# Own due times for the quarter products of two nested block products, other planning constants, one more sum by adding transfers, 19 warm-up products and a re-cut first block

## The chip, the cores and the metric

The kernel runs on one core of a Trainium2 chip. In the profile's words the core has PE (TensorE, the matrix engine; PEld are its weight loads), DVE (VectorE), ACT (ScalarE), POOL (GpSimd) and SP (SyncE, which here only issues transfers). Each engine takes its instructions in program order and waits on semaphores for the others. Transfers that SP, ACT and POOL issue run on 16 shared DMA engines. Operands lie in SBUF, products in eight PSUM banks of 128 x 512 floats. The metric is the device time of one execution in microseconds (us).

## The reference

```python
g = sigmoid((x * gate_w).sum(-1, keepdims=True))           # x: 2048 x 1024
a = x @ dft_hid_re.T;  b = x @ dft_hid_im.T
A = dft_seq_re @ a - dft_seq_im @ b                        # 2048 x 1024
h = layernorm(x)                                           # over the 1024 columns
u = gelu(h.T @ w1 + b1)                                    # 1024 x 3584
B = (u @ w2 + b2).T                                        # 2048 x 1024
out = g * A + (1 - g) * B
```

All inputs and the output are float32.

## The kernel before

Four stages follow each other: `Fourier` (names begin with q: the sequence transforms of x), `Mixed` (y: the hidden transforms of q, into the output), `Up` (u: normalised x times w1, gelu) and `Down` (o: times w2, added into the output). Each stage is a product of two matrices whose operands W and R are cut into blocks. A bilinear scheme of 26 block products (`SCHEME`) takes the place of the 32 that blocks of 4 x 4 and 4 x 2 would need: for each product j (in names p0 to p25, by its place in the stage's order) sums of blocks are made on DVE (L539 adds, L542 subtracts), multiplied, and the result is added from PSUM onto up to eight blocks of the output (`q_c`, `u_c`, ... ; L907 and L909 copy on ACT or DVE the first time, L915 adds on DVE afterwards). Sums that are needed again are kept in DRAM and loaded again.

A float32 block is split into a rounded part hi (ACT, L572; in the first block partly DVE, L570) and a rest lo = v - hi (DVE, L579, or L577 when the sign turns). PE multiplies hi x hi, lo x hi and hi x lo into the same PSUM bank (L863, L864, L865; L982 in the first block). One block product in stage q is four steps k = 0 to 3 along the contraction, each 4 x 2 banks x 3 products.

Stage q has three specialities that the change touches. (1) In its first product, p0, step k = 0 is cut by columns (`first`, L935), so that PE can begin on a part: W comes in columns 0:128, 128:256 and 256:512, R in 0:256, 256:512 and 512:1024. (2) Products p9 and p22 (`Q_NEST`) are computed by `nested` (L995): the block product is cut once more into seven quarter products (tags 1, 5, 6, 2, 7, 3, 4, L1040) in banks X, T, Z and V, with sums of quarters (`q_p22_r_s1`, `q_p22_w_t1`, ...) made on DVE. (3) For products in `Q_DMA` a sum of two R blocks isn't made on DVE: POOL issues a transfer that adds a block from DRAM onto the one in SBUF (`add_onto`, L548). There are four such transfers of 512 KB per product, one for each k.

Nothing in the code fixes the order of the instructions by hand. Every operation is a task of `Graph` with an engine, a cost in us and a key (the step of the product it belongs to). `dues` (L330) walks back from the order of the PE tasks and gives each task a time by which it has to be done: the due time of what uses it, less its own cost, less `WAIT`, and less `LOAD` for a transfer or `HOP` otherwise; a task may not be due later than five us after its key's step on PE, whatever uses it. `schedule` (L360) then plays the program through with assumed durations (a transfer takes its bytes / `DMA_RATE` one after the other, plus `DMA_LATENCY`); each engine takes, of the tasks that are ready and have a buffer, the one due first. Buffers are 40 slots of 4 KB per partition ("f") and 23 of 2 KB ("h"). An "h" tile may take an "f" slot (`has_slots`, L385) only if it is first in line and one "f" is free. The order that comes out is the order in which each engine gets its instructions.

At its start PE runs 13 products of constants (`warm_up`, L1379), which nothing reads.

Of the kernel before, what the change touches and what calls it, by code (L numbers as in the profile page):

```python
# [14 lines left out]
P = 128  # L15
# [123 lines left out]
Q_DMA = (23,)  # L139
# [147 lines left out]
class Graph:  # L287
# [72 lines left out]
    def schedule(self):  # L360
# [113 lines left out]
def gated_mix_kernel(  # L474
# [444 lines left out]
    class Fourier(Bilinear):  # L919
# [15 lines left out]
        first = {"W": [(0, P), (P, P), (2 * P, 2 * P)], "R": [(0, 2 * P), (2 * P, 2 * P), (H, H)]}  # L935

        def block(self, x_, b, j, k, key):

            if (j, k) != (0, 0):
                return super().block(x_, b, j, k, key)  # L940
            src, r = self.source(x_, b, k)
            b = Buf("f" if x_ == "R" else "h", f"q_{x_}{b}_p0_0", None, 3)
            for i, (c, n) in enumerate(self.first[x_]):
                load(-18 + 2 * i, View(b, c, n, i), src[:, c:c + n], queue="ACT" if x_ == "W" and i < 2 else "SP")
            return View(b, 0, self.n[x_])

# [12 lines left out]
        def matmuls(self, j, ks, ops, eps):  # L959

            if j or ks[0] > 1:
                return super().matmuls(j, ks, ops, eps)
            (rh, rl), (wh, wl) = ops[0]
            hh, hl, lh = (wh, rh), (wh, rl), (wl, rh)
            if ks == (0,):
                for m in range(4):
                    for n in range(2):
                        self.PS[m, n] = View(Buf("ps", f"ps_q_p0_{m}_{n}"), 0, H)
                todo = [(hh, (0,), 0, 1), (lh, (0,), 0, 1), (hh, (1,), 0, 1), (hh, (0, 1), 1, 2), (lh, (1,), 0, 1), (lh, (0, 1), 1, 2),
                        (hl, (0, 1), 0, 1), (hl, (0, 1), 1, 2), (hh, (2, 3), 0, 2), (hl, (2, 3), 0, 2), (lh, (2, 3), 0, 2)]  # L970
                todo += [(p, (0, 1, 2, 3), 2, 4) for p in (hh, lh, hl)]
            else:
                todo = [(p, (0, 1, 2, 3), n, n + 2) for n in (0, 2) for p in (hh, hl, lh)]
            fresh = {(m, n) for m in range(4) for n in range(2)} if ks == (0,) else set()
            for (w, r), ms, a, b in todo:
                some = [(m, self.PS[m, a // 2], (m, a // 2) in fresh) for m in ms]
                fresh -= {(m, a // 2) for m in ms}

                def go(_, w=w, r=r, a=a, b=b, some=some):
                    c0 = a // 2 * H  # L980
                    for m, bank, begin in some:
                        nc.tensor.matmul(bank.buf.t[:, a * 2 * P - c0:b * 2 * P - c0], w.ap[:, m * P:(m + 1) * P],  # L982
                                         r.ap[:, a * 2 * P:b * 2 * P], start=begin, stop=False, skip_group_check=True)

                wp = tuple(sorted({min(m, 2) for m in ms})) if ks == (0,) else None
                rp = (2 if a == 2 else tuple(range(a, b))) if ks == (0,) else None
                g.add({"PE": (0.227 if b - a == 2 else 0.12) * len(ms)}, step, go, r=((w.buf, wp), (r.buf, rp)),
                      w=[q.reg for _, q, _ in some])
# [6 lines left out]
        def nested(self, j):  # L995
# [3 lines left out]
            key, name = step, f"{self.name}_p{j}"  # L999
# [40 lines left out]
            def product(tag, bank, begin, end=False):  # L1040
                rv, wv = made_r[tag], made_w[tag]
                rh, rl = parts("R", tag, rv, [1, 1])
                wh, wl = parts("W", tag, wv, [a[1] * b[1] for a, b in zip(rv, wv)])
                for m, ps in enumerate(banks[bank]):

                    def go(_, m=m, ps=ps):
                        for i in range(2):
                            wc, rc = slice((2 * i + m) * P, (2 * i + m + 1) * P), slice(i * H, i * H + H)
                            for w, r in ((wh, rh), (wh, rl), (wl, rh)):
                                nc.tensor.matmul(ps.ap, w.ap[:, wc], r.ap[:, rc], start=begin and i == 0 and (w, r) == (wh, rh),  # L1050
                                                 stop=end and i == 1 and w is wl, skip_group_check=True)

                    g.add({"PE": 1.36}, step, go, r=(rh.buf, rl.buf, wh.buf, wl.buf), w=(ps.reg,))
# [11 lines left out]
            def out(c, i):  # L1065
                at = 2 - 2 * (c in "VT")
                for m, ps in enumerate(banks[c]):
                    self.PS[at + m, int(c in "XT")] = ps
                    self.read(j, at + m, int(c in "XT"), step + i, 1)

            product("1", "X", True)
            copy("X", banks["Z"])
            s1, t1 = plus("s1", "R", r21, r22), plus("t1", "W", w12, w11, True)
# [305 lines left out]
    def warm_up(_):  # L1379
        for n in range(13):  # L1380
            nc.tensor.matmul(pw.t[:, :2 * P], ones[:, :P], ones[:, :2 * P], start=True, stop=True)

    g.add({"PE": 3.0}, 0, warm_up, w=(pw,))
# [61 lines left out]
```

## Time and profile before

| | |
|---|---|
| runs (median of 3) | 1846.67 us (1847.55, 1846.67, 1846.49) |
| profiled execution, own time | 1847.67 us |
| its span, first to last instruction | 1845.9 us |
| busy: PE, DVE, ACT, POOL | 1838.4, 1716.2, 923.3, 246.9 us |
| granted TensorE clock | 1.000 |
| DMA | 491.89 MB, mean 266 GB/s over the span |

The profile shows one execution. Names in it are without numbers: `q_p_w_lo` stands for the lo part of W in any product of q. A row of the timeline has the start, the length, engine, line, operation, out<-in, the shape and the count of equal instructions merged into it, and in brackets the idle time before it and who ended it. Consecutive matmuls overlap by design: one of 512 columns is shown as 389 ns long, but the next starts 227 ns after it, and a busy PE is not one without delays. `PEq`, `SPq`, `POOLq` are queues that issue.

### The profile page before, as it was taken

The numbers are of one execution on the slowest core, as the hardware profiler recorded it, in microseconds if no ns is written. First come the engines' busy times: TensorE is split into PE (matmuls) and PEld (weight loads), VectorE is DVE, ScalarE is ACT, GpSimd is POOL, SyncE is SP. The second block draws the span as 40 slices with busy tenths as digits, with TensorE's granted clock in tenths as the row PEclk, the third lists the DMA queues.
The fourth block names the chain that finished last, engine by engine and source line by source line (L and its number), as shares of the span: only waits on it lengthen the run. The fifth ranks groups of instructions, "written<-read, shape, count | busy, mean of one in ns | idle before, by whom it ended". The sixth has DMA issues, their size and how long they took to land.

```text
span 1845.9 us, 24510 instructions
## 1 busy us (share of the span) xinstructions
PE 1838.4 (100%) x8113; PEld 1520.6 (82%) x8113; DVE 1716.2 (93%) x2506; ACT 923.3 (50%) x1444; POOL 246.9 (13%) x420
## 2 busy tenths in 40 slices
PE   9999999999999999999999999999999999999999
PEld 7888888888788888888888888888888888888887
DVE  8899899989999999999997799899899999989996
ACT  5443545644645545586554434355465435444543
POOL 0100010011122101112121211121120000001111
PEclk9999999999999999999999999999999999999999
DMA  9956577978799867989658798996998665675973
GB/s 372 351 196 266 200 286 288 349 256 332 240 327 311 254 195 256 329 293 323 240 190 298 266 334 322 333 375 219 368 311 276 175 223 179 208 210 141 287 196 85
DMA packets 200447, 491.89 MB, mean 266 GB/s; under 512 B 24768, under 2 KB 25792, under 8 KB 200320
## 3 DMA queue, kind: packets, MB, share of 16 engines
q1 hardware_dynamic: 161424, 371.88, 58.5%
q0 software_dynamic: 38464, 118.25, 19.7%
q8 instruction: 63, 1.03, 0.2%
q14 instruction: 64, 0.52, 0.1%
q10 hardware_dynamic: 432, 0.20, 0.0%
HBM read 375.41 MB, written 114.82 MB: 266 GB/s over the span
## 4 chain that ended last, share of the span: by engine, by line
PE 93%; DVE 4%; DMA 2%; issue 0%; ACT 0%; SPq 0%; DVEq 0%
PE ps_u_p L865 9%; PE ps_u_p L864 9%; PE ps_u_p L863 9%; PE ps_o_p L863 9%; PE ps_o_p L864 9%; PE ps_o_p L865 9%; PE ps_q_p L864 6%; PE ps_q_p L865 6%; PE ps_q_p L863 6%; PE ps_y_p L865 5%; PE ps_y_p L863 5%; PE ps_y_p L864 5%; PE ps_q_p_X L1050 1%; DVE q_p_r_lo L579 1%; DVE q_c L915 1%; DMA q_R_p<-q_R 1%
## 5 line engine op out<-in xcount | busy, mean ns | idle before, releaser
L864 PE MATMUL ps_u_p<-u_p_r_lo,u_p_w_hi 128*128 128x512 f32 x728 | 283.2, 389 | 0.0
L863 PE MATMUL ps_u_p<-u_p_r_hi,u_p_w_hi 128*128 128x512 f32 x728 | 283.2, 389 | 0.0
L865 PE MATMUL ps_u_p<-u_p_r_hi,u_p_w_lo 128*128 128x512 f32 x728 | 283.2, 389 | 0.0
L863 PE MATMUL ps_o_p<-o_p_r,o_p_w 128*128 128x512 f32 x726 | 282.5, 389 | 0.1
L865 PE MATMUL ps_o_p<-o_p_r,o_p_w 128*128 128x512 f32 x726 | 282.4, 389 | 0.0
L864 PE MATMUL ps_o_p<-o_p_r,o_p_w 128*128 128x512 f32 x726 | 282.4, 389 | 0.0
L863 PE MATMUL ps_q_p<-q_p_r_hi,q_p_w_hi 128*128 128x512 f32 x592 | 230.3, 389 | 0.0
L864 PE MATMUL ps_q_p<-q_p_r_lo,q_p_w_hi 128*128 128x512 f32 x592 | 230.3, 389 | 0.0
L865 PE MATMUL ps_q_p<-q_p_r_hi,q_p_w_lo 128*128 128x512 f32 x592 | 230.3, 389 | 0.0
L572 ACT ACTIVATE q_p_r_hi<-q_R_p 128x1024 fp32r<-128x1024 f32 (+1 forms) x104 | 102.8, 1002 | 133.2 <-DVE q_R_p L539 97.8
L572 ACT ACTIVATE u_p_w_hi<-u_W_p 128x896 fp32r<-128x896 f32 x104 | 97.9, 950 | 139.2 <-DVE u_W_p L539 39.9
L572 ACT ACTIVATE o_p_r<-o_R_p 128x512 fp32r<-128x512 f32 x175 | 107.4, 626 | 113.0 <-DVE o_R_p L542 36.9
L572 ACT ACTIVATE o_p_w<-o_W_p 128x512 fp32r<-128x512 f32 x182 | 111.8, 626 | 102.4 <-PE ps_o_p L865 38.4
L863 PE MATMUL ps_y_p<-y_p_r,y_p_w 128*128 128x512 f32 x416 | 162.1, 390 | 0.0
L864 PE MATMUL ps_y_p<-y_p_r,y_p_w 128*128 128x512 f32 x416 | 161.9, 389 | 0.0
L865 PE MATMUL ps_y_p<-y_p_r,y_p_w 128*128 128x512 f32 x416 | 161.8, 389 | 0.0
L864 PEld LDWEIGHTS ps_u_p<-u_p_r_lo,u_p_w_hi 128*128 128x128 f32 x728 | 136.6, 188 | 28.5
L863 PEld LDWEIGHTS ps_u_p<-u_p_r_hi,u_p_w_hi 128*128 128x128 f32 x728 | 136.6, 188 | 28.3
L865 PEld LDWEIGHTS ps_u_p<-u_p_r_hi,u_p_w_lo 128*128 128x128 f32 x728 | 136.6, 188 | 28.3
L863 PEld LDWEIGHTS ps_o_p<-o_p_r,o_p_w 128*128 128x128 f32 x726 | 136.3, 188 | 28.7 <-DVE o_c L915 0.5
L865 PEld LDWEIGHTS ps_o_p<-o_p_r,o_p_w 128*128 128x128 f32 x726 | 136.3, 188 | 28.5
L864 PEld LDWEIGHTS ps_o_p<-o_p_r,o_p_w 128*128 128x128 f32 x726 | 136.3, 188 | 28.1
(229 smaller groups left out, 3641.4 us busy)
## 6 DMA issues: line engine op xcount, KB each, us to landing
q_R_p<-in_ct_dram SPq DMA_DIRECT2D x127, 512.0 KB, 7.7
u_W_p<-in_w_dram SPq DMA_DIRECT2D x136, 448.0 KB, 6.3
o_W_p<-in_w_dram SPq DMA_DIRECT2D x196, 256.0 KB, 5.1
o_R_p<-u SPq DMA_DIRECT2D x140, 256.0 KB, 4.4
u<-u_c POOLq DMA_DIRECT2D x126, 256.0 KB, 5.9
y_W_p<-q SPq DMA_DIRECT2D x99, 256.0 KB, 5.1
q<-q_c POOLq DMA_DIRECT2D x80, 256.0 KB, 6.1
q_W_p<-in_x_dram SPq DMA_DIRECT2D x75, 256.0 KB, 7.2
```

Source lines behind the costliest of these rows:

```text
L572: g.add({"ACT": act(v.n)}, key, lambda e: nc.scalar.activation(hi.ap, v.ap, AF.Copy, scale=-1.0 if negate else 1.0), r=(v.reg,), w=(hi.reg,))
L579: nc.vector.tensor_sub(lo.ap, v.ap, hi.ap.bitcast(F32))
L863: nc.tensor.matmul(bank.ap, wh.ap[:, c], rh.ap[:, e], start=a, stop=False, skip_group_check=True)
L864: nc.tensor.matmul(bank.ap, wh.ap[:, c], rl.ap[:, e], start=False, stop=False, skip_group_check=True)
L865: nc.tensor.matmul(bank.ap, wl.ap[:, c], rh.ap[:, e], start=False, stop=b, skip_group_check=True)
L915: lambda e: nc.vector.scalar_tensor_tensor(o.ap, ps.ap, scale, o.ap, op0=ALU.mult, op1=ALU.add),
L1050: nc.tensor.matmul(ps.ap, w.ap[:, wc], r.ap[:, rc], start=begin and i == 0 and (w, r) == (wh, rh), stop=end and i == 1 and w is wl, skip_g ...
```

## The change

Five edits go together.

- The planner's constants: `HOP` 0.3 to 0.2, `DMA_RATE` 330e3 to 360e3, `LOAD` 8 to 11, `WAIT` 0.5 to 1.5. And `has_slots` lets any "h" tile take an "f" slot if eight are free (`SPARE`), where it was one, and only for the tile first in line. These change the order on every engine.
- In `nested`, the tasks of the seven quarter products had all one key, that of the product's first step. Now the i-th has the key `base + 4 * i / 7`, so that operands of the later quarters are due later.
- `Q_DMA` gets product 20 besides 23: the sum of blocks 0 and 12 of R for p20 is made by four adding transfers onto the tile that p19 has loaded (`q_R0_p19`).
- In p0, step 0, W comes as columns 0:128 and 128:512 (both issued by ACT); PE does first all of row block 0 in the first half, then row blocks 1 to 3. R of step 1 is loaded and split in two halves.
- Warm-up: 19 products in place of 13.

```diff
-HOP = 0.3
-DMA_RATE = 330e3
+HOP = 0.2
+DMA_RATE = 360e3
+SPARE = 8
-LOAD, WAIT, NEAR, FAR = 8.0, 0.5, 0.45, 3.0
+LOAD = 11.0
+WAIT = 1.5
...
-Q_DMA = (23,)
+Q_DMA = (20, 23)
...
-                    if b.kind != "h" or waiting["h"][0] is not t or len(free["f"]) - bisect_left(waiting["f"], t) < 1:
+                    spare = 1 if waiting["h"][0] is t else SPARE
+                    if b.kind != "h" or len(free["f"]) - bisect_left(waiting["f"], t) < spare:
                         return False
...
-        first = {"W": [(0, P), (P, P), (2 * P, 2 * P)], "R": [(0, 2 * P), (2 * P, 2 * P), (H, H)]}
+        def parts(self, x_, j, k):
+
+            if (j, k) == (0, 0):
+                return [(0, P), (P, 3 * P)] if x_ == "W" else [(0, 2 * P), (2 * P, 2 * P), (H, H)]
+            return [(0, H), (H, H)] if (x_, j, k) == ("R", 0, 1) else None
...
-                load(-18 + 2 * i, View(b, c, n, i), src[:, c:c + n], queue="ACT" if x_ == "W" and i < 2 else "SP")
+            for i, (c, n) in enumerate(parts):
+                load(key if k else i - 9, View(b, c, n, i), src[:, c:c + n], queue="SP" if k or x_ == "R" else "ACT")
...
-                todo = [(hh, (0,), 0, 1), (lh, (0,), 0, 1), (hh, (1,), 0, 1), (hh, (0, 1), 1, 2), (lh, (1,), 0, 1), (lh, (0, 1), 1, 2),
-                        (hl, (0, 1), 0, 1), (hl, (0, 1), 1, 2), (hh, (2, 3), 0, 2), (hl, (2, 3), 0, 2), (lh, (2, 3), 0, 2)]
-                todo += [(p, (0, 1, 2, 3), 2, 4) for p in (hh, lh, hl)]
+                todo = [(hh, one, 0, 1, True), (lh, one, 0, 1, False), (hh, one, 1, 2, False), (lh, one, 1, 2, False),
+                        (hl, one, 0, 1, False), (hh, rest, 0, 2, True), (hl, rest, 0, 2, False), (lh, rest, 0, 2, False),
+                        (hl, one, 1, 2, False), (hh, every, 2, 4, True), (hl, every, 2, 4, False), (lh, every, 2, 4, False)]
...
+            def at(i):
+
+                nonlocal key
+                key = base + 4 * i / 7
...
-                    g.add({"PE": 1.36}, step, go, r=(rh.buf, rl.buf, wh.buf, wl.buf), w=(ps.reg,))
+                    g.add({"PE": 1.36}, key, go, r=(rh.buf, rl.buf, wh.buf, wl.buf), w=(ps.reg,))
...
+            at(4)
             made_r["7"], made_w["7"] = plus("s3", "R", r11, r21, True), plus("t3", "W", w22, w12, True)
             product("7", "X", False)
             sum_of("T", "X")
-            out("T", 3)
+            out("T")
+            at(5)
             made_r["3"] = plus("s4", "R", r12, s2, True)
...
-        for n in range(13):
+        for n in range(19):
...
-    g.add({"PE": 3.0}, 0, warm_up, w=(pw,))
+    g.add({"PE": 4.05}, 0, warm_up, w=(pw,))
```

How the order moves is shown at three places. In these rows the line, the operation, out<-in and the shape of what is written stand; numbers at the end of a name only count tiles.

First, the start of PE, after the warm-up products. Names `ps_q_p_0_0` to `ps_q_p_3_1` are the banks of row block 0 to 3 and column half 0 or 1. Before:

```order
L982 MATMUL ps_q_p_0_0_340<-q_p_r_hi,q_p_w_hi 128x256
L982 MATMUL ps_q_p_0_0_340<-q_p_r_hi,q_p_w_lo 128x256
L982 MATMUL ps_q_p_1_0_345<-q_p_r_hi,q_p_w_hi 128x256
L982 MATMUL ps_q_p_0_0_340<-q_p_r_hi,q_p_w_hi 128x256
L982 MATMUL ps_q_p_1_0_345<-q_p_r_hi,q_p_w_hi 128x256
L982 MATMUL ps_q_p_1_0_345<-q_p_r_hi,q_p_w_lo 128x256
L982 MATMUL ps_q_p_0_0_340<-q_p_r_hi,q_p_w_lo 128x256
```

The same place now:

```order
L993 MATMUL ps_q_p_0_0_348<-q_p_r_hi,q_p_w_lo 128x256
L993 MATMUL ps_q_p_0_0_348<-q_p_r_lo,q_p_w_hi 128x256
L993 MATMUL ps_q_p_1_0_357<-q_p_r_hi,q_p_w_hi 128x512
L993 MATMUL ps_q_p_2_0_358<-q_p_r_hi,q_p_w_hi 128x512
L993 MATMUL ps_q_p_3_0_359<-q_p_r_hi,q_p_w_hi 128x512
L993 MATMUL ps_q_p_1_0_357<-q_p_r_lo,q_p_w_hi 128x512
```

Before, twelve products of 256 columns use row blocks 0 and 1, and row blocks 2 and 3 follow with six of 512. Now five products of 256 columns use row block 0 alone, and nine of 512 follow for row blocks 1 to 3. ACT, which issues the W transfers and makes the hi parts, before:

```order
L546 DMA q_W_p_0_272<-in_x_dram 128x128 x2
L572 ACT_TABLE_LOAD
L572 ACTIVATE q_p_w_hi<-q_W_p_0_272 128x128 x2
L572 ACTIVATE q_p_r_hi<-q_R_p_0_274 128x512
L572 ACTIVATE q_p_w_hi<-q_W_p_0_272 128x256
L572 ACTIVATE q_p_r_hi<-q_R_p_1_280 128x1024
```

And now:

```order
L551 DMA q_W_p_0_278<-in_x_dram 128x128
L551 DMA q_W_p_0_278<-in_x_dram 128x384
L577 ACT_TABLE_LOAD
L577 ACTIVATE q_p_w_hi<-q_W_p_0_278 128x128
L577 ACTIVATE q_p_w_hi<-q_W_p_0_278 128x384
L577 ACTIVATE q_p_r_hi<-q_R_p_0_280 128x512
L577 ACTIVATE q_p_w_hi<-q_W_p_1_285 128x512
L577 ACTIVATE q_p_r_hi<-q_R_p_1_287 128x512
```

The second half of W came from SP's queue behind 512 KB of R, and its hi part stood behind that of R; now all of W comes over ACT's queue, and its hi part stands ahead.

Second, DVE just before the nested product p22. `q_c7` rows read the banks of the product before (`ps_q_p18_...`, the banks of a chain p18 to p21); the others prepare quarters of p22. Before:

```order
L577 SCALAR_TENSOR_TENSOR q_p22_w_7_lo_4391<-q_p22_w_t3_4310,q_p22_w_7_hi_4324 128x512
L579 TENSOR_TENSOR q_p22_r_4_lo_4397<-q_R15_p21_2_3936,q_p22_r_4_hi_4201 128x512
L579 TENSOR_TENSOR q_p22_r_4_lo_4397<-q_R15_p21_3_3970,q_p22_r_4_hi_4201 128x512
L577 SCALAR_TENSOR_TENSOR q_p22_w_4_lo_4408<-q_p22_w_t4_4321,q_p22_w_4_hi_4345 128x512
L577 SCALAR_TENSOR_TENSOR q_p22_w_2_lo_4411<-q_W5_p19_2_3519,q_p22_w_2_hi_4245 128x256
L577 SCALAR_TENSOR_TENSOR q_p22_w_2_lo_4411<-q_W5_p19_3_3568,q_p22_w_2_hi_4245 128x256
L577 SCALAR_TENSOR_TENSOR q_p22_w_3_lo_4429<-q_W5_p19_2_3519,q_p22_w_3_hi_4319 128x256
L577 SCALAR_TENSOR_TENSOR q_p22_w_3_lo_4429<-q_W5_p19_3_3568,q_p22_w_3_hi_4319 128x256
L915 SCALAR_TENSOR_TENSOR q_c7_2_3209<-ps_q_p18_1_1_3658,q_c7_2_3209 128x512
L915 SCALAR_TENSOR_TENSOR q_c7_4_3235<-ps_q_p18_2_0_3668,q_c7_4_3235 128x512
L915 SCALAR_TENSOR_TENSOR q_c7_4_3235<-ps_q_p18_2_1_3674,q_c7_4_3235 128x512
```

Now, from the same bank on:

```order
L920 SCALAR_TENSOR_TENSOR q_c7_2_3236<-ps_q_p18_1_1_3671,q_c7_2_3236 128x512
L584 TENSOR_TENSOR q_p22_r_4_lo_4354<-q_R15_p21_3_3921,q_p22_r_4_hi_4228 128x512
L920 SCALAR_TENSOR_TENSOR q_c7_4_3261<-ps_q_p18_2_0_3679,q_c7_4_3261 128x512
L1332 SCALAR_TENSOR_TENSOR xg14_4376,zg_72<-x14_4084,gw_2351 128x1024
L920 SCALAR_TENSOR_TENSOR q_c7_4_3261<-ps_q_p18_2_1_3683,q_c7_4_3261 128x512
L547 TENSOR_TENSOR q_p22_w_t4_4393<-q_W5_p19_2_3496,q_p22_w_t2_4246 128x256
L920 SCALAR_TENSOR_TENSOR q_c7_6_3283<-ps_q_p18_3_0_3688,q_c7_6_3283 128x512
L547 TENSOR_TENSOR q_p22_w_t4_4393<-q_W5_p19_3_3536,q_p22_w_t2_4246 128x256
L544 TENSOR_TENSOR q_W5_p19_0_3412<-q_W12_p23_0_4204,q_W5_p19_0_3412 128x512
L920 SCALAR_TENSOR_TENSOR q_c7_6_3283<-ps_q_p18_3_1_3692,q_c7_6_3283 128x512
L584 TENSOR_TENSOR q_p22_r_3_lo_4416<-q_p22_r_s4_4296,q_p22_r_3_hi_4321 128x1024
```

The bank reads stood behind the whole preparation of p22; now they alternate with it, and w_t4 (two rows), r_3_lo, w_3_lo (two rows) and w_4_lo come after the read of bank `ps_q_p18_2_1`, while one `xg` row has come ahead of it. Further up DVE's queue the four sums for p20 (`q_R12_p20` + `q_R0_p19`, each 128x1024) are gone.

Third, DVE in stage u, where the sum of two loaded W blocks for step 3 of p19 (`u_W6_p19_3` + `u_W5_p19_3`) stands. Before:

```order
L539 TENSOR_TENSOR u_W6_p19_1_10745<-u_W6_p19_1_10745,u_W5_p19_1_10784 128x896
L915 SCALAR_TENSOR_TENSOR u_c4_6_10471<-ps_u_p17_6_0_10733,u_c4_6_10471 128x512
L577 SCALAR_TENSOR_TENSOR u_p19_w_0_lo_10868<-u_W6_p19_0_10690,u_p19_w_0_hi_10829 128x896
L579 TENSOR_TENSOR u_p19_r_1_lo_10877<-h9_7142,u_p19_r_1_hi_10782 128x512
L577 SCALAR_TENSOR_TENSOR u_p19_w_1_lo_10884<-u_W6_p19_1_10745,u_p19_w_1_hi_10866 128x896
L539 TENSOR_TENSOR u_W6_p19_2_10786<-u_W6_p19_2_10786,u_W5_p19_2_10788 128x896
L579 TENSOR_TENSOR u_p19_r_2_lo_10897<-h10_7164,u_p19_r_2_hi_10857 128x512
L579 TENSOR_TENSOR u_p19_r_3_lo_10901<-h11_7285,u_p19_r_3_hi_10879 128x512
L539 TENSOR_TENSOR u_W6_p19_3_10799<-u_W6_p19_3_10799,u_W5_p19_3_10818 128x896
```

And now:

```order
L920 SCALAR_TENSOR_TENSOR u_c4_0_10442<-ps_u_p17_0_0_10694,u_c4_0_10442 128x512
L582 SCALAR_TENSOR_TENSOR u_p19_w_0_lo_10804<-u_W6_p19_0_10633,u_p19_w_0_hi_10788 128x896
L920 SCALAR_TENSOR_TENSOR u_c4_0_10442<-ps_u_p17_1_0_10706,u_c4_0_10442 128x512
L544 TENSOR_TENSOR u_W6_p19_3_10756<-u_W6_p19_3_10756,u_W5_p19_3_10770 128x896
L920 SCALAR_TENSOR_TENSOR u_c4_2_10499<-ps_u_p17_2_0_10713,u_c4_2_10499 128x512
L920 SCALAR_TENSOR_TENSOR u_c4_2_10499<-ps_u_p17_3_0_10721,u_c4_2_10499 128x512
```

Before, the sum stood behind all seven reads of the banks `ps_u_p17_...`; now five of these reads stand behind the sum, and so behind the landing of its two loads.

Counted over the program, PE has 8116 products (8113 before: six more of warm-up, three fewer in p0), DVE 18 more first-time copies out of PSUM and four sums fewer, ACT 18 copies fewer, and four transfers of 512 KB have gone from SP to POOL.

More of the change, by code (lines that the diff above doesn't have):

```diff
@@ L964, in matmuls @@
             hh, hl, lh = (wh, rh), (wh, rl), (wl, rh)
+            one, rest, every = (0,), (1, 2, 3), (0, 1, 2, 3)
             if ks == (0,):
@@ L980, in go @@
+            for (w, r), ms, a, b, begin in todo:
+                banks = [self.PS[m, a // 2] for m in ms]
+                def go(_, w=w, r=r, ms=ms, a=a, b=b, begin=begin, banks=banks):
                     c0 = a // 2 * H
-                    for m, bank, begin in some:
+                    for m, bank in zip(ms, banks):
                         nc.tensor.matmul(bank.buf.t[:, a * 2 * P - c0:b * 2 * P - c0], w.ap[:, m * P:(m + 1) * P],
                                          r.ap[:, a * 2 * P:b * 2 * P], start=begin, stop=False, skip_group_check=True)
-                wp = tuple(sorted({min(m, 2) for m in ms})) if ks == (0,) else None
@@ L986, in matmuls @@
-                rp = (2 if a == 2 else tuple(range(a, b))) if ks == (0,) else None
-                g.add({"PE": (0.227 if b - a == 2 else 0.12) * len(ms)}, step, go, r=((w.buf, wp), (r.buf, rp)),
-                      w=[q.reg for _, q, _ in some])
+                wp = None if ks != (0,) else 0 if ms == one else 1 if ms == rest else (0, 1)
+                rp = a // 2 if ks != (0,) else 2 if a == 2 else tuple(range(a, b))
+                g.add({"PE": (0.227 if b - a == 2 else 0.12) * len(ms)}, step, go, r=((w.buf, wp), (r.buf, rp)), w=[q.reg for q in banks])
@@ L1068, in out @@
                     self.PS[at + m, int(c in "XT")] = ps
-                    self.read(j, at + m, int(c in "XT"), step + i, 1)
+                    self.read(j, at + m, int(c in "XT"), key + 4 / 7, 1)
             product("1", "X", True)
             copy("X", banks["Z"])
+            at(1)
             s1, t1 = plus("s1", "R", r21, r22), plus("t1", "W", w12, w11, True)
```

40 lines of the change are left out of this document (21 added, 19 removed).

## The prediction

> **What bounds the kernel.** I read the page's summary first, then the chain that ended last, then PE's waits. From the page of before:
>
> ```profile
> span 1845.9 us, 24510 instructions
> PE 1838.4 (100%) x8113; PEld 1520.6 (82%) x8113; DVE 1716.2 (93%) x2506; ACT 923.3 (50%) x1444; POOL 246.9 (13%) x420
> GB/s 372 351 196 266 200 286 288 349 256 332 240 327 311 254 195 256 329 293 323 240 190 298 266 334 322 333 375 219 368 311 276 175 223 179 208 210 141 287 196 85
> HBM read 375.41 MB, written 114.82 MB: 266 GB/s over the span
> PE 93%; DVE 4%; DMA 2%; issue 0%; ACT 0%; SPq 0%; DVEq 0%
> ```
>
> PE is busy for all but 7.5 us of the span, and the last row, the chain's shares, is 93% PE; the rows between are what the DMA engines moved, in 40 slices and on average. What the change can win is therefore what PE idles, and some slow first products; what it can lose has no such limit. PE's own waits, "waited for: us in total, times, longest":
>
> ```profile
> PE ps_q_p_T L1050 <- DVE q_c L915: 1.7, 1, 1.7
> PE ps_q_p L982 <- ACT q_p_w_hi L572: 1.3, 1, 1.3
> PE pw L1381 <- PEq L1432: 0.8, 1, 0.8
> ```
>
> Two waits can move: one in the nested p22, one in p0. The third is PE's own beginning and stays. So I read the timeline around both. First the start (start, length, engine, line, operation, names, shape):
>
> ```profile
> 0.78 2.93 PE L1381 MATMUL pw<-const-bfloat16-1.0 128*128 128x256 bf16 x13 [0.78 <-PEq L1432]
> ...
> 3.81 0.53 PE L982 MATMUL ps_q_p<-q_p_r_hi,q_p_w_hi 128*128 128x256 f32 x1
> 3.95 0.31 ACT L572 ACTIVATE q_p_w_hi<-q_W_p 128x128 fp32r<-128x128 f32 x1 [0.19 <-DMA q_W_p<-in_x_dram]
> ...
> 4.36 0.57 PE L982 MATMUL ps_q_p<-q_p_r_hi,q_p_w_hi 128*128 128x256 f32 x3
> ...
> 6.29 0.63 ACT L572 ACTIVATE q_p_r_hi<-q_R_p 128x512 fp32r<-128x512 f32 x1 [2.04 <-DMA q_R_p<-in_ct_dram]
> 6.83 0.40 ACT L572 ACTIVATE q_p_w_hi<-q_W_p 128x256 fp32r<-128x256 f32 x1
> 6.96 0.69 DVE L579 TENSOR_TENSOR q_p_r_lo<-q_R_p,q_p_r_hi 128x512 fp32r<-128x512 f32 x1 [1.79 <-ACT q_p_r_hi L572]
> 7.28 0.30 PEld L982 LDWEIGHTS ps_q_p<-q_p_r_hi,q_p_w_hi 128*128 128x128 f32 x2 [1.52 <-ACT q_p_w_hi L572]
> ...
> 7.57 0.42 DVE L579 TENSOR_TENSOR q_p_w_lo<-q_W_p,q_p_w_hi 128x256 fp32r<-128x256 f32 x1
> 8.68 1.06 ACT L572 ACTIVATE q_p_r_hi<-q_R_p 128x1024 fp32r<-128x1024 f32 x1 [1.45 <-DMA q_R_p<-in_ct_dram]
> 8.78 1.07 PE L982 MATMUL ps_q_p<-q_p_r_hi,q_p_w_hi 128*128 128x512 f32 x4
> ...
> 11.50 1.07 PE L982 MATMUL ps_q_p<-q_p_r_hi,q_p_w_hi 128*128 128x512 f32 x4
> ```
>
> A row of n merged products shows the overlap of the last; from start to start it is 2.72 us from 8.78 to 11.50 for the 12 products of a column half, so 0.227 us for 512 columns and half of that, 0.113, for 256. Of PE's time before 8.78, 1.5 us is the wait that ends at 7.28: ACT took the 512 columns of R as they landed (6.29) and only then W's columns 256:512 (6.83), for which row blocks 2 and 3 waited. Then the end of stage q:
>
> ```profile
> 440.00:460.00 20.00, 20.00 (x90) 16.57 (x89) 20.00 (x22) 7.52 (x10) 0.94 (x2) 1.00 0.70 265
> 460.00:475.00 15.00, 15.00 (x68) 12.43 (x67) 15.00 (x29) 13.08 (x25) 1.81 (x2) 1.00 0.38 102
> 475.00:490.00 15.00, 13.28 (x58) 10.62 (x57) 15.00 (x26) 6.56 (x11) 1.74 (x2) 1.00 0.86 235
> ```
>
> These are stretches with the busy time of PE, PEld, DVE, ACT and POOL, the granted clock (1.00), DMA share and GB/s. DVE has no idle moment from 440 to 490 while PE has none until the third stretch: DVE has fallen behind, and PE pays at the end. How, from DVE's and PE's timelines:
>
> ```profile
> 440.08 4.62 DVE L539 TENSOR_TENSOR q_R_p<-q_R_p,q_R_p 128x1024 f32<-128x1024 f32 x4
> ...
> 477.13 3.48 DVE L579 TENSOR_TENSOR q_p_r_lo<-q_p_r_s,q_p_r_hi 128x1024 fp32r<-128x1024 f32 x3
> ...
> 484.75 1.43 DVE L577 SCALAR_TENSOR_TENSOR q_p_w_lo<-q_W_p,q_p_w_hi 128x256 fp32r<-128x256 f32 x4
> 486.09 2.48 DVE L915 SCALAR_TENSOR_TENSOR q_c<-ps_q_p,q_c 128x512 f32<-128x512 f32 x4
> ```
>
> ```profile
> 485.91 0.39 PE L1050 MATMUL ps_q_p_T<-q_p_r_hi,q_p_w_lo 128*128 128x512 f32 x1
> 488.03 0.50 PE L1050 MATMUL ps_q_p_T<-q_p_r_hi,q_p_w_hi 128*128 128x512 f32 x1 [1.73 <-DVE q_c L915]
> 488.37 0.40 PE L1050 MATMUL ps_q_p_T<-q_p_r_lo,q_p_w_hi 128*128 128x512 f32 x1
> ```
>
> PE's next product was due 0.227 after 485.91, at 486.14; it started at 488.03, 1.89 later, and took 0.34 instead of 0.227 to the next start: 2.0 us in all. The bank it needed was read by `q_c` at 486.09 and on, the reads that the order of DVE has behind all operands of p22. Elsewhere PE loses little: the largest such place has a late load at its root (first row from the chain, the others from PE's timeline):
>
> ```profile
> 1652.12 8.36 DMA o_W_p<-o_W
> ```
>
> ```profile
> 1672.22 0.39 PE L865 MATMUL ps_o_p<-o_p_r,o_p_w 128*128 128x512 f32 x1
> 1672.67 0.50 PE L863 MATMUL ps_o_p<-o_p_r,o_p_w 128*128 128x512 f32 x1
> 1673.01 0.39 PE L864 MATMUL ps_o_p<-o_p_r,o_p_w 128*128 128x512 f32 x1
> ```
>
> The loss is (1672.67 - 1672.22 - 0.227) + 0.11 = 0.34.
>
> **The change: the start.** The 13 warm-up products take 2.93, the last one's full length among it; from start to start that is between 0.20 ((2.93 - 0.53) / 12, with the length of the product at 3.81) and 0.225 (2.93 / 13). I take 0.213: 19 of them end at 0.78 + 4.05 = 4.83. Before, the first real product started at 3.81, so the first products come 1.0 later. Then come five products of 256 columns (0.57) and nine of 512 (2.04), and one of 256 (0.11): column half 0 ends at 7.55 if no operand is late. Before, it ended at 8.78. That is the most that the start can give: 1.2. The operands: W's columns 128:512 now follow W's first part on ACT's queue. Its 64 KB were there for the row at 3.95; 192 KB have 128 KB more. At the 372 GB/s of the first slice that is 0.35 us, at half of it, as R moves at the same time, 0.7; I estimate a landing L at 4.65. From L: ACT's hi of 384 columns 0.5 (between 0.40 for 256 and 0.63 for 512 columns), DVE's lo 0.55 (between 0.42 and 0.69), DVE's lo of R's second 256 columns 0.42, which DVE does next: 6.1. The three lo products of row blocks 1 to 3 stand fourth on; PE gets to them at 4.83 + 0.57 + 0.68 = 6.1. So up to L = 4.65 the start gives 1.2, and each us later costs one. Worst: W's second part comes only as R's columns 512:1024 do, at 6.29; then half 0 ends at 6.29 + 1.47 + 6 x 0.227 + 0.11 = 9.2, a loss of 0.45. I take -1.2, in the range -1.2 to +0.45. Step 1 then starts at 10.3 instead of 11.5. Its operands: R came whole, for the row at 8.68; now W and R's first half are issued ahead with as many bytes in front, so hi of both is done by 8.7 + 2 x 0.6 = 9.9; R's second half, behind 512 KB more, is wanted 2.7 after 10.3. Halving R costs issue only. 0.
>
> By the Trainium skill, "TensorE: Matmul & The Clock Gate", "What's actually happening", the clock rises after about 3.4 us of activity, whatever the number of products. Here one product of 256 columns at 3.81 has 0.53 and three after 4.36 have 0.57 together, so the trace agrees. By that rule the last three of 19 would be fast, warm-up would end at 4.5 instead of 4.83 and the sum would be up to 0.3 lower. Against the edit speaks "DMA: Bandwidth & Descriptors", "Issuing engines are not separate DMA queues": transfers of ACT and SP interleave on the same engines, and issuing from two saves only issue time; by that, L would be later, towards the loss. "Queues, rings and completion order" in the same page has them served in turn, which gives L near 4.65. No run here shows which holds.
>
> **p20's sums and p22.** The four sums are of the kind in the row at 440.08: 4.62 / 4 = 1.155 each, 4.6 us less on DVE ahead of p22, in a stretch where DVE never idles. Behind the bank read that PE waits for have gone, by the front part's rows, w_t4 (2), r_3_lo, w_3_lo (2) and w_4_lo; with 1.16 for r_lo (3.48 / 3), 0.36 for a row of 256 columns (1.43 / 4) and 0.6 for one of 512, 0.72 + 1.16 + 0.72 + 0.6 = 3.2. One `xg` row has come ahead, as long as an r_lo, 1.16. The read comes 4.6 + 3.2 - 1.2 = 6.6 us earlier in DVE's work, for a stall of 2.0: -2.0, with some cover to spare. Bounds: -2.0 (a wait can't go below nothing) and 0. What is late next is DVE's w_3 and w_4, now behind the read: the quarters 3 and 4 are the last of seven, some 5.4 us and more after T. Of the transfers:
>
> ```profile
> q_R_p<-in_ct_dram POOLq DMA_DIRECT2D x4, 512.0 KB, 9.7
> q_R_p<-in_ct_dram SPq DMA_DIRECT2D x28, 512.0 KB, 8.6
> ```
>
> (issued by POOL or SP from 380 to 500, us to landing.) An adding transfer takes 9.7, where SP's load takes 8.6, and reads as many bytes; POOL's stores queued behind it wait that little longer. The adds stand some 35 DVE rows ahead of use, over 20 us at 0.6 and more each, so 9.7 is hidden: 0. If that cover were gone each of four would be late by at most 9.7 less what is left.
>
> **Planning times and copies.** The 18 copies that go from ACT to DVE are like these:
>
> ```profile
> L909 DVE TENSOR_SCALAR q_c<-ps_q_p 128x512 f32<-128x512 f32 x12 | 8.0, 686 | 2.7 <-PE ps_q_p L865 2.5
> L539 DVE TENSOR_TENSOR u_W_p<-u_W_p,u_W_p 128x896 f32<-128x896 f32 x80 | 85.4, 1083 | 9.3 <-DMA u_W_p<-in_w_dram 9.3
> ```
>
> (busy us, mean ns, idle before and its releaser.) 18 x 0.69 = 12 us of DVE, against 1845.9 - 1716.2 = 130 us idle there; 0 outside 420 to 490. The second row has what the new order risks: DVE already idles 9.3 us in stage u for loads, and PE loses nothing by it. In the front part's third place the sum of two loads moves ahead of five bank reads of 0.6. If its loads are late, reads of banks wait behind it, and then PE for banks. Transfers here:
>
> ```profile
> u_W_p<-in_w_dram SPq DMA_DIRECT2D x8, 448.0 KB, 8.3
> 1180.00:1190.00 10.00, 10.00 (x46) 8.29 (x45) 8.07 (x11) 3.68 (x7) 1.53 (x3) 1.00 1.01 387
> ```
>
> (1180 to 1200.) Loads take 8.3 with the DMA engines full, while DVE has 2 us idle in 10 to catch up. Price of such a wait: nearest is 1672.67, 0.34. I count one more than go: +0.4, in -0.34 (none, and 1672's gone) to +3 (nine). `SPARE` and the cheaper `HOP` only move order; in that count.
>
> Sum: -1.2 - 2.0 + 0.4 = -2.8. The profiled execution took 1847.67 for a span of 1845.9 and is 1.0 above the median, so: span 1843.1, its own time 1844.9, median 1843.9.
>
> **The rivals.** (1) The start gives nothing: L at 5.85 or later, by the service of queues or a slow ACT. For it: R's 512 columns landed as late as 6.29. Against: ACT's two transfers landed before SP's third. -2.8 + 1.2: 1845.1. (2) p22's wait stays, since DVE remains full to 490 with the 12 us of copies partly there, or an add is late. Against: 6.6 us for 2.0. 1845.9. (3) Slower: sums of loads moved up on DVE meet loads that are not there, in u and o, place of the third piece. At 0.34 each the 3.2 us gained are used up by ten waits (3.2 / 0.34); at 17 of the 52 products of u and o it is -3.2 + 5.8 = +2.6: 1849.3. For it: 8.3 us landings, full DMA engines, a larger `DMA_RATE` than the 266 GB/s mean, so loads planned to land too soon. Against: the 9.3 us in the row above cost PE nothing, and loads are planned longer ahead (11 for 8). (4) All goes well, without new waits: -1.2 - 2.0 - 0.34 = -3.5: 1843.1.
>
> **How the numbers follow.** Forecast 0.57 (1843.9, itself 1843.2 to 1844.8); (1) 0.15; (2) 0.07; (3) 0.13; (4) 0.08. The range leaves out below 1842.5 (less than 0.1) and above 1846.8, where most of (3) lies. A measurement here can't tell less than about 0.2%, 3.7 us: faster means under 1843.0, part of (4) and the forecast's edge, 0.09; slower is above 1850.4, half of (3), 0.07; the rest is 0.84.
>
> **What would show it.** Right: PE's list of waits without the T row; column half 1 of p0 starting near 7.6 and step 1 near 10.3; the gap at 488 gone, DVE still full there; L near 4.65 by ACT's hi of 384 columns. Wrong: ACT's 384 columns after 5.9; a PE wait on `q_R_p` or on an add near p20; several PE starts 0.34 late in u and o, with DVE idle for DMA well above 9.3 in the u_W row.

## The result, and the profile after

The changed kernel takes 1859.76 us (median of six runs, 1854.86 to 1861.22) against 1846.97 (six runs, 1846.18 to 1847.55): a ratio of 1.0066, interval 1.0053 to 1.0079. It is slower by 13 us, 0.7%, where 3 us less were forecast. Its runs also scatter over 6 us, where those of before scatter over 1.4. The profiled execution took 1861.22, so 1.5 above the median. From its page, and PE's list of waits:

```profile
span 1859.5 us, 24530 instructions
PE 1847.0 (99%) x8116; PEld 1520.5 (82%) x8116; DVE 1714.1 (92%) x2520; ACT 913.6 (49%) x1426; POOL 251.4 (14%) x424
HBM read 375.41 MB, written 114.82 MB: 264 GB/s over the span
```

```profile
PE ps_q_p L868 <- DVE q_c L920: 2.9, 3, 2.2
PE ps_o_p L868 <- DVE o_c L920: 2.4, 9, 0.7
PE ps_u_p L868 <- DVE u_c L920: 1.5, 5, 0.5
PE pw L1402 <- PEq L1453: 0.8, 1, 0.8
PE ps_y_p L868 <- DVE y_c L920: 0.7, 3, 0.2
PE ps_o_p L868 <- ACT o_p_r L577: 0.6, 1, 0.6
```

The two waits that the prediction set out to remove are not there. In their place PE waits in all four stages, for one kind of work nearly everywhere: DVE's reads of banks (`q_c`, `y_c`, `u_c`, `o_c`). The list counts only idle time, not the slow products after it. From PE's timeline, adding up what lies above 0.227 from start to start of products of 512 columns (0.113 for 256) from 20 us on, PE loses 16.9 us: 5.0 in q (from 420 to 426), 1.6 in y, 3.6 in u, 6.6 in o. Before it was 2.6: 2.0, 0.3, 0, 0.3. The difference is 14.3, and the start gained 0.85, which leaves 13.5 of the 13.6 us between the spans.

At the start the operands came about as early as forecast, and PE gained less than forecast:

```profile
0.78 4.21 PE L1402 MATMUL pw<-const-bfloat16-1.0 128*128 128x256 bf16 x19 [0.78 <-PEq L1453]
...
4.61 0.53 ACT L577 ACTIVATE q_p_w_hi<-q_W_p 128x384 fp32r<-128x384 f32 x1 [0.92 <-DMA q_W_p<-in_x_dram]
...
5.64 0.42 DVE L584 TENSOR_TENSOR q_p_r_lo<-q_R_p,q_p_r_hi 128x256 fp32r<-128x256 f32 x1
...
7.90 1.09 PE L993 MATMUL ps_q_p<-q_p_r_hi,q_p_w_hi 128*128 128x512 f32 x4
...
10.65 1.07 PE L993 MATMUL ps_q_p<-q_p_r_hi,q_p_w_hi 128*128 128x512 f32 x4
```

W's 384 columns landed by 4.61 (4.65 was estimated), column half 1 starts at 7.90 instead of 8.78 and step 1 at 10.65 instead of 11.50: 0.85 gained of the 1.2. The rest went to PE's first products, which still ran slowly (below).

The largest new loss, near 420, by DVE, by PE, and in stretches of 1 us (the number behind the five engines' busy times, 0.98 or 0.50, is the granted clock):

```profile
412.60 3.67 DVE L920 SCALAR_TENSOR_TENSOR q_c<-ps_q_p,q_c 128x512 f32<-128x512 f32 x6
417.85 1.23 DVE L584 TENSOR_TENSOR q_p_r_lo<-q_R_p,q_p_r_hi 128x1024 fp32r<-128x1024 f32 x1 [1.58 <-ACT nmean L1329]
418.99 6.06 DVE L920 SCALAR_TENSOR_TENSOR q_c<-ps_q_p,q_c 128x512 f32<-128x512 f32 x10
```

```profile
417.74 0.39 PE L870 MATMUL ps_q_p<-q_p_r_hi,q_p_w_lo 128*128 128x512 f32 x1
420.33 0.50 PE L868 MATMUL ps_q_p<-q_p_r_hi,q_p_w_hi 128*128 128x512 f32 x1 [2.20 <-DVE q_c L920]
...
424.33 0.63 PE L870 MATMUL ps_q_p<-q_p_r_hi,q_p_w_lo 128*128 128x512 f32 x1
424.76 0.63 PE L868 MATMUL ps_q_p<-q_p_r_hi,q_p_w_hi 128*128 128x512 f32 x1
```

```profile
421.00:422.00 1.00, 0.77 (x4) 0.43 (x3) 1.00 (x3) 0.00 (x0) 0.35 (x2) 0.98 1.05 426
422.00:423.00 1.00, 0.81 (x3) 0.08 (x1) 1.00 (x3) 0.00 (x0) 0.89 (x3) 0.50 1.02 418
424.00:425.00 1.00, 1.00 (x4) 0.81 (x3) 1.00 (x3) 0.00 (x0) 0.25 (x1) 0.50 1.03 414
```

Six of the sixteen bank reads are done, then one row that prepares p20 (`r_lo`) stands still for 1.6 us with ten reads behind it, and PE waits 2.2 for the next bank. Before, all sixteen reads stood in one piece:

```profile
409.55 9.65 DVE L915 SCALAR_TENSOR_TENSOR q_c<-ps_q_p,q_c 128x512 f32<-128x512 f32 x16
```

The waiting row's named releaser ended at 417.0, so it was another. A transfer fits: POOL's stores of R blocks (`q_R<-q_R_p`) free slots that p20's tiles take. In the plan that `schedule` makes of this kernel, `q_p20_r_0_hi` takes the slot of `q_R23_p18_2` and `q_p20_r_0_lo`, the row that stands, the slot of `q_R23_p18_3`; POOL's two stores are the last users of these.

```profile
q_R<-q_R_p POOLq DMA_DIRECT2D x2, 512.0 KB, 8.7
q_R_p<-in_ct_dram POOLq DMA_DIRECT2D x2, 512.0 KB, 12.4
```

(issues from 403 to 408, median us to landing.) The first store, issued at 404.7, took 6.0, and ACT's r_hi, which waited for it, starts at 410.78. The second, issued at 406.4, took 11.3, so it landed at 417.7, just ahead of the waiting row at 417.85; the plan had given it 9.3. In the same stretch of before the one such store took 6.1 and there was no adding transfer. Here one adding transfer (10.6) was issued between the stores and one (14.1) behind them, and a load that SP issued at 406.2 took 10.9 as well: 3584 KB were issued in these 5 us instead of 2048, and the DMA engines moved 390 GB/s instead of 398. So the second store was late with everything beside it; that POOL's queue itself held it up is not shown. The clock then adds to the loss: it falls to 0.50 at 422, the products from there take 0.43 from start to start instead of 0.227, and of the 5.0 us lost some 1.3 are that.

In stage u the mechanism of the third rival stands in the rows:

```profile
1175.78 2.48 DVE L920 SCALAR_TENSOR_TENSOR u_c<-ps_u_p,u_c 128x512 f32<-128x512 f32 x4
1181.91 1.09 DVE L544 TENSOR_TENSOR u_W_p<-u_W_p,u_W_p 128x896 f32<-128x896 f32 x1 [3.65 <-DMA u_W_p<-in_w_dram]
1182.92 0.68 DVE L920 SCALAR_TENSOR_TENSOR u_c<-ps_u_p,u_c 128x512 f32<-128x512 f32 x1
```

```profile
1183.66 0.50 PE L868 MATMUL ps_u_p<-u_p_r_hi,u_p_w_hi 128*128 128x512 f32 x1 [0.54 <-DVE u_c L920]
```

DVE stands 3.65 us before the sum of two loads that aren't there, with a bank read behind it whose end PE waits for. By the plan's order this is the sum for step 0 of p19. The place that was shown ahead of the prediction, the sum for step 3 (1196.50 in this trace), doesn't wait; the same pattern hit elsewhere. Over the kernel, DVE's own list of waits has these as its greatest changes, first of before, then of after:

```profile
DVE u_W_p L539 <- DMA u_W_p<-in_w_dram: 9.3, 3, 5.7
DVE o_W_p L539 <- DMA o_W_p<-in_w_dram: 5.0, 5, 1.9
DVE q_R_p L542 <- DMA q_R_p<-in_ct_dram: 1.3, 1, 1.3
```

```profile
DVE u_W_p L544 <- DMA u_W_p<-in_w_dram: 18.0, 12, 3.7
DVE q_R_p L547 <- DMA q_R_p<-in_ct_dram: 12.8, 4, 7.8
DVE o_W_p L544 <- DMA o_W_p<-in_w_dram: 12.4, 14, 2.2
```

All rows of that list with a transfer as releaser add up to 29 us before and 62 after. This sum, "DVE's waits for transfers", is given for each experiment.

### The profile page after: what moved, and what is told of

The parts are those of the page before. It is cut to its first block, busy times and chain, and to the rows that moved or that the text cites. A ratio compares the mean times of both kernels' runs of the same rounds, so it can differ in the third digit from the quotient of the medians.

```text
span 1859.5 us, 24530 instructions
## 1 busy us (share of the span) xinstructions
PE 1847.0 (99%) x8116; PEld 1520.5 (82%) x8116; DVE 1714.1 (92%) x2520; ACT 913.6 (49%) x1426; POOL 251.4 (14%) x424
```

## The experiments

Theory A: the planning constants put sums on DVE ahead of loads that haven't landed. Theory B: the edits in stage q, the adding transfers first, push everything behind them. The first four runs tell these apart. "PE's loss" is that from 20 us on, by stage; times are medians, with the ratio to before and its interval. The ratios go by runs of before taken alongside, whose medians were 1847.0 to 1847.3. A loss is that of the one profiled execution, which lies up to 3.2 us from the median of its kernel.

**The constants of before in the changed kernel.**

```diff
-HOP = 0.2, DMA_RATE = 360e3, SPARE = 8, LOAD = 11.0, WAIT = 1.5
+HOP = 0.3, DMA_RATE = 330e3, SPARE = 99, LOAD = 8.0, WAIT = 0.5
```

> The changed kernel with the five planning constants of before (HOP, DMA_RATE, LOAD, WAIT and the rule for spare slots); the edits in stage q stay. Theory A (the constants order DVE's sums ahead of loads that have not landed, and bank reads wait behind them): PE's new losses in stages y, u and o, 11.8 us in the trace of the changed kernel (1.6 + 3.6 + 6.6), go; the 5.0 us near 420 belong to the adding transfers of p20 and stay: 1848. If the stall near 420 needs the constants too: 1843. Theory B (the adding transfers and the new order in q push everything behind them): still 1855 to 1860.

1853.14, ratio 1.0032 (1.0020 to 1.0044). PE's loss: q 5.0, y 2.2, u 0, o 1.4; DVE's waits for transfers 23. The losses of u and o went, as theory A has it; that of y did not. But a new 5.0 came up at 513, in a product behind p22 that uses its banks, with other releasers than near 420, and the time is none of those expected:

```profile
PE ps_q_p_V L869 <- DVE q_p_r_lo L584: 2.3, 1, 2.3
PE ps_q_p_V L868 <- ACT q_p_r_hi L577: 0.5, 1, 0.5
```

**The new constants alone, in the kernel before.**

```diff
-HOP 0.3, DMA_RATE 330e3, LOAD 8.0, WAIT 0.5, old rule for slots
+HOP 0.2, DMA_RATE 360e3, LOAD 11.0, WAIT 1.5, SPARE 8
```

> The kernel before with the new planning constants alone (HOP 0.2, DMA_RATE 360e3, LOAD 11, WAIT 1.5, SPARE 8), no edit in stage q. Theory A: about 12 us of new PE waits in y, u and o, behind DVE that waits for loads: 1857 to 1860. Theory B: within 2 us of before, 1845 to 1849.

1853.74, ratio 1.0033 (1.0021 to 1.0045). PE's loss: q 1.0, y 0.7, u 3.2, o 3.1; DVE's waits for transfers 64. Theory B is out for y, u and o: no edit of stage q is in this kernel. About half of the slowdown is there, less than theory A expected. In this trace 1.9 us more are lost ahead of 20 us: PE waits 1.7 for the hi part of W's second half where it waited 1.3, products then start 0.43 apart until 11.3, and step 1 of p0 starts at 13.42 instead of 11.50.

**The changed kernel without p20's adding transfers.**

```diff
-Q_DMA = (20, 23)
+Q_DMA = (23,)
```

> The changed kernel with Q_DMA = (23,), so the sums for p20 are made by DVE again. Theory A: only the stall near 420 (5.0 us) can go: 1855; the wait in p22 may come back in part (up to +2). Theory B: the losses of y, u and o go as well: 1843 to 1847.

1854.30, ratio 1.0034 (1.0021 to 1.0047). PE's loss: q 0, y 1.3, u 3.2, o 6.9. The stall near 420 went, and that alone, by 5.0; the wait at 488 didn't come back.

**WAIT alone back.**

```diff
-WAIT = 1.5
+WAIT = 0.5
```

> The changed kernel with WAIT alone back at 0.5. Theory A1 (of the constants WAIT is the cause: each link of a chain from sum to hi and lo to product moves an operand 1 us ahead, a bank read has one link only, so reads of banks fall behind sums): as with all constants of before, 1843 to 1848. Theory A2 (DMA_RATE or LOAD is the cause, loads being planned to land earlier than they do): stays at 1856 to 1860.

1852.21, ratio 1.0030 (1.0018 to 1.0043). PE's loss: q 0, y 1.6, u 0.4, o 6.1; waits for transfers 46. In part only, between the two expectations: WAIT alone isn't the root. That the stall near 420 is gone with the adding transfers still there says that it needs them and the order both.

Then `DMA_RATE`, `LOAD` and `SPARE`, one at a time, and the rate alone in the kernel before. `HOP` was not taken back alone.

```diff
-DMA_RATE = 360e3
+DMA_RATE = 330e3
```

> The changed kernel with DMA_RATE alone back at 330e3. PE's losses in y, u and o were 11.8 us in the changed kernel, 1.4 with all constants of before, 8.1 with WAIT alone back. Theory R (the planner takes loads to land sooner than they do, and puts sums on DVE ahead of reads): losses in y, u and o at most 4 and DVE's waits for loads of u_W near 9 us, as before; about 1850 or less. If another constant is the cause: they stay at 8 to 12, about 1855 to 1860.

1845.91, ratio 0.9993 (0.9984 to 1.0002). This one constant takes all 14 us away. PE's loss: q 0, y 0.1, u 0, o 1.6; waits for transfers 25. PE's list has two rows left:

```profile
PE pw L1402 <- PEq L1453: 0.8, 1, 0.8
PE ps_o_p L868 <- DVE o_c L920: 0.6, 3, 0.2
```

p20's adding transfers are in it, as are LOAD 11 and WAIT 1.5, and they cost nothing that shows at this rate.

```diff
-LOAD = 11.0
+LOAD = 8.0
```

> The changed kernel with LOAD alone back at 8. Theory L (a load due 11 us ahead is issued early, more are under way at once, each takes longer, and what is needed first waits): losses in y, u and o at most 4. Theory R: they stay at 8 to 12 or grow, since loads are asked for later.

1856.62, ratio 1.0056 (1.0039 to 1.0073); PE's loss q 0.1, y 2.4, u 5.4, o 2.1, waits for transfers 71. Theory L is out. (The profiled execution is 2.7 below this median.)

```diff
-SPARE = 8
+SPARE = 99
```

> The changed kernel with the old rule for spare slots. Theory S (small tiles take the large slots early, and loads of large tiles wait for a slot): losses in y, u and o at most 4. Theories R and L: they stay at 8 to 12.

1861.26, ratio 1.0075 (1.0060 to 1.0090); PE's loss q 0, y 1.7, u 5.3, o 10.3, waits 66. Theory S is out.

```diff
 (the kernel before)
-DMA_RATE = 330e3
+DMA_RATE = 360e3
```

> The kernel before with DMA_RATE 360e3 alone. Theory R: DVE's waits for loads of u_W and o_W grow from 14 to 25 us or more and PE loses 4 us or more in y, u and o, where it lost 0.5: 1850 or more. Otherwise: under 1.5 lost, 1846 to 1848.

1849.19, ratio 1.0011 (1.0002 to 1.0021); waits for transfers 46 instead of 29, but PE's loss 3.2 instead of 2.6. The waits grow as theory R says, by less than the changed kernel shows, and the loss is between the two expectations. So the higher rate needs some of the other new constants beside it to do its harm; which of them was not separated.

A constant that works at one value may be a lucky draw, so it was moved further in both directions, all else as in the changed kernel.

> The changed kernel with DMA_RATE 300e3. Theory R (the rate that the planner assumes is over what loads get, so sums stand too early on DVE): a lower rate only gives loads more time; losses of PE in y, u and o at most 2 us and DVE's waits for loads no more than with 330e3 (u_W and o_W 13 us together); 1844 to 1847. Theory C (any other constant draws a new order, and 330e3 was a lucky one): 1849 or more is as likely.

> The changed kernel with DMA_RATE 345e3. Theory R: between 330e3 (1845.9) and 360e3 (1859.8), 1848 to 1856. Theory C: anywhere from 1845 to 1862.

> The changed kernel with DMA_RATE 390e3. Theory R: more waits of DVE for loads than at 360e3 (u_W and o_W over 30 us together) and 1860 to 1872. Theory C: anywhere from 1845 to 1862.

| DMA_RATE | median us | ratio, interval | DVE's waits for transfers | for PE | PE's loss q, y, u, o |
|---|---|---|---|---|---|
| 300e3 | 1863.79 | 1.0087 (1.0070 to 1.0103) | 2 | 106 | 5.6, 5.1, 0, 9.0 |
| 330e3 | 1845.91 | 0.9993 (0.9984 to 1.0002) | 25 | 60 | 0, 0.1, 0, 1.6 |
| 345e3 | 1849.39 | 1.0011 (1.0001 to 1.0020) | 50 | 44 | 0, 0, 2.1, 1.3 |
| 360e3 | 1859.76 | 1.0066 (1.0053 to 1.0079) | 62 | 41 | 5.0, 1.6, 3.6, 6.6 |
| 390e3 | 1885.35 | 1.0202 (1.0185 to 1.0219) | 89 | 36 | 0.4, 4.3, 16.8, 15.9 |

DVE's waits for transfers rise in order with the assumed rate, as theory R says and theory C does not. From 330e3 up the time follows them (at 390e3 further than the 1860 to 1872 expected). Below, theory R failed: at 300e3 DVE hardly ever waits for a load and PE is 18 us slower. There PE waits for operands instead of banks (from PE's list at 300e3, then at 390e3):

```profile
PE ps_y_p L868 <- ACT y_p_w L577: 2.9, 1, 2.9
PE ps_o_p L869 <- DVE o_p_r L584: 2.9, 1, 2.9
PE ps_o_p L868 <- ACT o_p_r L577: 2.2, 1, 2.2
```

```profile
PE ps_u_p L868 <- DVE u_c L920: 9.5, 13, 4.2
PE ps_o_p L868 <- DVE o_c L920: 9.1, 8, 6.0
```

The column of waits for PE runs the other way. At 300e3 DVE's longest is at 1346, and PE's two longest waits in stage o follow it:

```profile
1346.03 0.69 DVE L920 SCALAR_TENSOR_TENSOR u_c<-ps_u_p,u_c 128x512 f32<-128x512 f32 x1 [10.72 <-PE ps_u_p L870]
```

DVE stands 10.72 us with a bank read first in line, then works almost without a pause, and PE waits for operands at 1356 and 1360. So the rate is a balance: too high, sums stand before their loads and bank reads behind them; too low, the reads stand first, and hi, lo and PE come late. That the rows behind this read could have run in those 10 us is the likely reading and wasn't tested. Of the 19.7 us that PE loses at 300e3, between 3 and 4 are products of 0.43 after its longest stops.

Theory C isn't empty either: any change of a constant draws a new order. At 330e3 two other kernels are 5 to 6 us slower than before, most of it in q: the one with all constants of before (1853.14) and the one with p20's adding transfers alone (1852.49, below). In u and o the rate separates the kernels. The eight traces at 330e3 lose 0.3 to 2.4 us there, the six at 360e3 with other new constants beside it 6.3 to 15.6, and the kernel before with 360e3 alone 1.6.

**The edits of stage q.** With the rate back the adding transfers were left out as well.

> The changed kernel with DMA_RATE 330e3 and Q_DMA = (23,): the sums for p20 on DVE again. If the quarters' own due times alone remove the wait at 488: no loss of PE between 400 and 500, and 1845 to 1847. If the adding transfers are needed for it: 1 to 2 us lost there again, 1846.5 to 1849. The start (step 1 of p0 near 10.6) is the same in both.

1845.90, ratio 0.9992 (0.9983 to 1.0001); no loss from 400 to 500. The adding transfers are not needed for it and worth nothing here. Then each edit of q alone in the kernel before, and the last kernel once more:

> The kernel before with the new start alone (re-cut step 0 of p0, halves of R in step 1, 19 warm-up products). Step 1 of p0 started 0.85 earlier in the changed kernel. If that holds alone and nothing behind it moves: 1846.2. If the median of the kernel is set by waits further on, the new order there decides: step 1 starts near 10.6 and the total still differs by up to 3 either way.

1846.54, ratio 0.9995 (0.9986 to 1.0004): step 1 starts at 10.96; PE's loss from 20 us on is 2.5, about as before. The three edits of the start were not tried one by one.

> The kernel before with the own due times of the quarter products alone. If they are what removes the wait of 2.0 at 488: 1845. If operands of late quarters, due later, come too late with WAIT 0.5 and LOAD 8 (with these and the adding transfers PE lost 5.0 in p22 and 2.2 near 600): a wait on r_lo or hi of a late quarter, 1849 to 1853.

1847.23, ratio 1.0001 (0.9992 to 1.0009): the wait at 488 is gone, and PE loses 2.0 near 595, in stage y, to waits for ACT (L572) and DVE (L579). What the edit gains in q it loses there, and the time is neither of the two expected.

> The kernel before with p20's four adding transfers alone. If 4.6 us less work on DVE end the wait at 488: 1845. If the read stays behind all operands of p22, or the reads of p20's sums only move: the wait stays, 1846.5 to 1847.5. If the adds hold up POOL's stores as in the changed kernel near 420: 1 to 5 us lost before 440.

1852.49, ratio 1.0027 (1.0017 to 1.0038): slower, and none of the three expectations came. The wait at 488 grew, with a half-rate clock behind it (PE), since DVE didn't use the time it was given (DVE's list of waits between 395 and 490):

```profile
490.37 0.76 PE L1050 MATMUL ps_q_p_T<-q_p_r_hi,q_p_w_hi 128*128 128x512 f32 x1 [4.03 <-DVE q_c L915]
490.93 0.63 PE L1050 MATMUL ps_q_p_T<-q_p_r_lo,q_p_w_hi 128*128 128x512 f32 x1
```

```profile
DVE q_p_w_lo L577 <- PE ps_q_p L864: 4.1, 1, 4.1
DVE q_c L915 <- PE ps_q_p L865: 2.0, 2, 1.8
DVE q_p_r_lo L579 <- ACT q_p_r_hi L572: 1.7, 2, 1.2
```

Four sums fewer on DVE became 7.8 us of waiting from 395 to 490, where it was 1.6 (1.3 and 0.3), for PE to let go of an operand's tile among others, and the reads still stand behind all of p22's preparation, now ending 2.3 later (DVE's four reads start at 488.42 instead of 486.09).

> The changed kernel with DMA_RATE 330e3 and without p20's adding transfers, once more with five rounds, since three gave 0.9992 with an interval that holds 1. If the start and p22 really gain 2.9 and the waits in o cost 1.0: 1845.3 to 1846.0, an interval under 1. Otherwise 1846.5 or more.

1846.74, ratio 0.9995 (0.9986 to 1.0004). This is the kernel of the run before these three, which had 1845.90: the same kernel differs by 0.8 from one set of runs to the next. A kernel that clearly beats the one before isn't among these; the best are equal to it within what can be measured.

## Why the prediction was wrong

- **The step that failed** is the term for new waits on loads: "I count one more than go: +0.4, in -0.34 (none, and 1672's gone) to +3 (nine)". Measured: +16.3, since PE's loss from 20 us on is 16.9, and of the 2.6 of before 0.6 is left without the wait at 488. 11.8 of the 16.9 are in y, u and o and belong to this term; the 5.0 in q belong to p20's transfers (below). Both factors were too small: PE's list has 18 waits in y, u and o where one more was counted, and 11.8 us are 0.65 for each where 0.34 was taken. The price came from a single place where DVE was just late. When DVE stands before a missing load, several bank reads are late one after the other, and each costs its own wait and a slow product (four times 0.5 us from 1221 to 1225). The number was judged from "the 9.3 us in the row above cost PE nothing". Those were three waits (ending at 989, 1017 and 1026) with no bank read in the rows just behind them. The prediction's own sign of this error came: the u_W row stands at 18.0.
- Rival 3 had the mechanism and its cause: "a larger `DMA_RATE` than the 266 GB/s mean, so loads planned to land too soon". The runs bear it out: with this constant alone taken back the kernel is at 1845.91. Its chance of 0.13 and its price were the error: at 0.34 each, 11.8 us in y, u and o would have been 35 waits. What the rival leaves out is that the rate doesn't do it alone (1849.19 in the kernel before) and that the opposite error costs as much (1863.79 at 300e3).
- "LOAD 11 for 8" was taken as protection. Taking it back, with the rate left, gives 1856.62, 3 us less and within the scatter of the two kernels, so no protection shows at this rate.
- p20's adding transfers: "9.7 is hidden: 0" was wrong near 420, by 5.0. The operand itself was there; what was late is a store that had to free a slot, one of those of which the text said "wait that little longer": 11.3 where 6.1 stood. With the new constants that meets a DVE row moved ahead of ten bank reads. With `LOAD`, `WAIT`, `SPARE` or the rate taken back, the same transfers cost 0.1 us or nothing in q.
- p22: "-2.0" came as forecast, but not for the reason in the sum. Of the 6.6 us of earlier reading, 4.6 were to come from the four sums. With the adding transfers alone the wait grows to 5.9 lost, and without them it is gone. The own due times do it. DVE time freed ahead of a place isn't time gained at that place.
- The start: -1.2 forecast, -0.85 in the profile, and 0.7 in the median of the start alone, below what can be told from none. The estimated L of 4.65 held (4.61). The term that was mis-sized is "five products of 256 columns (0.57)": they took 1.08, from 4.64 to 5.72, since the clock was still low; the warm-up products before them ended 0.2 sooner than estimated. By the Trainium skill, "DMA: Bandwidth & Descriptors", "Queues, rings and completion order", queues are served in turn; the landing at 4.61 ahead of R's third part (hi at 5.88) agrees, but no run here has the same transfer on SP's queue, so it doesn't show that ACT's queue was needed for it. By "TensorE: Matmul & The Clock Gate" of the Trainium skill, "What's actually happening", the clock would be up by 4.2, an estimate from 0.78 and its 3.4 us. Here 19 warm-up products and the next few stay slow: products of 256 columns start at 5.00, 5.21, 5.43, still 0.21 apart, and 0.11 apart only from 5.61, 4.8 after the first product. That page of the Trainium skill adds that its window runs freely and that the point so varies by 0.5 us; the 1.4 us here are more than that. It does vary: in the run with `LOAD` back, with the same start, products are 0.11 apart from 4.84 on.

## What to carry to other kernels

A planner that orders engines by assumed landing times needs its transfer rate checked against the trace: here a rate 9% above the best one tried cost 14 us, and one 9% below it cost 18. When an order changes, look at what stands behind each sum of loaded blocks on its engine; if it is the read of a bank that PE needs next, a late load can cost PE several waits, not one. An engine that waits for loads at no cost in the old order says nothing about the new one.

## What the hardware showed unexpectedly

A stall of PE can cost more than its length. After 1.9 us of standing (488, before) the clock stayed at 1.00. After a wait of 2.2 us and one of 0.2 it fell to 0.50 at 422 and stayed there until 425, and after 4.2 us (488, with the adding transfers alone) products took 0.43 instead of 0.227 for about 3 us, some 1.5 us more lost. Length alone doesn't decide it: in the kernel before with the new constants a wait of 1.7 that ended at 7.59 was enough for 0.50 from 8 to 10. Runs also scatter more in the changed kernel, whose DVE waits more on loads: over 6 us, where before it is 1.4.
